# Recurrent attention and gated block on one core: four steps of 3072 TensorE instructions, one turn by DMA, extra rows in 8, 1 and 7

## Chip, core and metric

One core of a Trainium2 chip runs the kernel. The metric is the device time of one execution in microseconds. Execution times are given as the median of several runs with the lowest and the highest. A profile is one further execution, whose own time stands beside its span.

## What is computed

A sequence of 2048 rows of 640 values goes through a layer norm, a recurrent attention with a small memory, and a gated two-layer block. The attention works through 64 segments of 32 rows, and the first 8 output rows of a segment are the memory that the next one begins with:

```python
for s in range(n_seg):                       # 64 segments of 32 rows
    h = concat([mem, xs], axis=1)            # 8 memory rows + 32 rows
    q, k, v = (einsum('btd,dhe->bhte', h, W) for W in (Wq, Wk, Wv))   # 32 heads of 128
    p = softmax(where(mask, einsum('bhqe,bhke->bhqk', q, k) * scale, -1e9))
    o = einsum('bhte,hed->btd', einsum('bhqk,bhke->bhqe', p, v), Wo)
    mem = o[:, :M]; outs.append(o[:, M:])
...
h  = x + attention(layernorm(x))
h2 = h + ((relu_gate(xn @ W_gate) * (xn @ W_up)) @ W_down)            # xn = layernorm(h)
```

## The kernel before

The program is recorded as a list of operations with the tiles that they read and write (class `_Graph`), a pass works out the semaphore waits, and each engine then runs its own operations in the order in which they were recorded. So the order of the source is the order of each engine's queue. Bank conflicts in PSUM count as dependencies too.

The 64 segments are the steps `s` of one loop. The 8 memory rows and 24 of the 32 rows make one block of 32 rows (`act_r`); the last 8 rows of four segments are put together into another block of 32 rows (`act_e`), whose K, Q and V products are made once per four steps as filler ("extra units", three of the four steps), and whose output products (`woe_pass`, the extra rows' Wo passes) fill the step with s%4 = 1.

Weights are the moving operand. `project` (line 365) multiplies one block of 32 rows by half of a weight matrix, 2048 columns: five chunks of the 640 input values, and for each chunk four products of 512 columns, `g` = 0 to 3, one on each quarter (32 columns) of the TensorE array, one PSUM quarter each. `pe.matmul` issues a weight load (the block of 32 rows is the stationary operand) and a product; `again` (line 357) issues the product alone, with the weights that are still in the quarter. With `held` the first chunk of a pass uses `again`, because the pass before ended with the same chunk: the second half of K and of Q goes through the chunks backwards (`WAYS`, line 925), and V begins with the chunk that Q ended with.

One step records, on TensorE, in this order: K in two halves (P2, P3); `pv_x` (line 646) of the step before, the products of the 24 and extra rows with the values; Q in two halves (P0, P1); V's first half with the `scores` (line 456) of the first half of the heads between its chunks; V's second half with the other scores; `pv_mem` (line 511) for the memory rows of the first half; the filler's first part; `pv_mem` of the second half; the filler's second part; `wo_split` (line 570), the Wo pass over the first half of the heads, with 320 columns per product; `wo_pass` (line 557) over the second half, with 160 columns; the filler's last part. DVE and ACT then turn the result into the next step's memory rows (`fold_split`, `to_act_split`), and the next step's K reads them.

In the steps with s%4 = 1 the filler is `woe_pass`, 16 groups of four products of 320 columns, cut by `WPARTS` (line 778) into 7, 2 and 7 groups. In the same steps the next 128 layer-normed rows are turned: `flip_rows` (line 345) issues a DMA transpose on SyncE's queue into `at`, and GpSimd copies the pieces into `act_r` and `act_e` (`ln1_back`, line 415). In step 57 only 64 rows are left; there `ln1_trans` (line 412) turns them with five TensorE transposes into a PSUM bank, and ACT copies them to `at`.

Ahead of the loop the first step's Wo passes go group by group as the pieces of Wo arrive. `keep_busy` (line 873) records products whose result nobody reads (16 per call with argument 4, on the quarters in turn) between them.

Of the kernel before, what the change touches and what calls it, by code (L numbers as in the profile page):

```python
# [26 lines left out]
class _Graph:  # L27
# [10 lines left out]
    def add(self, eng, fn, r=(), w=(), dma=False):  # L38
        if eng == "pool" and not dma:
            r, w = tuple(r) + (("pool",),), tuple(w) + (("pool",),)  # L40
        op = _Op(eng, fn, tuple(r), tuple(w), dma)
        self.ops.append(op)
        return op
# [120 lines left out]
def build_kernel(nc, A_x, A_mem0, A_Wq, A_Wk, A_Wv, A_Wo, A_seg_len, B_W_gate, B_W_up, B_W_down, out):  # L164
    _, S, D = A_x.shape
# [6 lines left out]
    DC = D // 128  # L172
# [22 lines left out]
    W = ar.alloc("W", [128, 3, DC, HD], BF16)  # L195
# [52 lines left out]
    xl = ar.alloc("xl", [128, D], BF16)  # L248
    at = ar.alloc("at", [128, D], BF16)
# [6 lines left out]
    def bank(b):  # L256
        return ps[:, b * 512:(b + 1) * 512]

    def bank_bf(b):
        return ps[:, b * 512:(b + 1) * 512].bitcast(BF16)  # L260

    BQ = (0, 1)
    T0, T1 = 2, 3
    P0, P1, P2, P3 = 4, 5, 6, 7
# [10 lines left out]
    def B(n):  # L275
        return ("B", n)
# [7 lines left out]
    for i in range(2):  # L284
        add("dve", lambda v, i=i: v.memset(oT[i][:], 0.0), w=[("oT", i, n, kh) for n in "mx" for kh in range(2)])
        add("pool", lambda p, i=i: p.memset(act_r[i][:], 0.0),
            w=[("act", i, j, "m") for j in range(4)] + [("act", i, "x")] + [("act", i, "x", j) for j in range(4)])
# [6 lines left out]
    for g in range(4):  # L294
        for j in range(4):
            for r in range(2):
                sl, n = mca[32 * g:32 * g + 32, j, r, :], 0 if r == g % 2 else 1 + j
# [47 lines left out]
    def flip_rows(dst, src, skey, dkey):  # L345

        add("sp", lambda e: e.dma_start_transpose(dst, src[:, :]), r=[skey], w=[dkey], dma=True)

    def transpose_rows(src, skey, n, b):
        def f(pe):  # L350
            for c in range(DC):
                i = pe.matmul(bank_bf(b)[:, c * 128:c * 128 + n], src[0:n, c * 128:(c + 1) * 128], ident[0:n, 0:n],
                              is_transpose=True)
            return i
        add("pe", f, r=[skey, ("ident",)], w=[B(b)])

    def again(pe, dst, lhsT, rhs, start, stop, g):

        return pe.add_instruction(mybir.InstMatmult(  # L359
            name=nc.get_next_instruction_name(), engine=mybir.EngineType.PE,  # L360
            ins=[pe.lower_ap(rhs), pe.lower_ap(lhsT)], outs=[pe.lower_ap(dst)], start_tensor_calc=start,
            stop_tensor_calc=stop, tile_size=(128, 32 if g is not None else 128), tile_position=(0, 32 * (g or 0)),
            bass_skip_group_check=True, ldweights=False))

    def project(act, akeys, j, halves, banks, chunks=range(5), ends=(0, DC - 1), held=False):
        swap = 1 if j == 2 and akeys[0][0] == "acte" else 0

        def f(pe):
            for c in chunks:
                for n, i in enumerate(halves):  # L370
                    for g in range(4):
                        o = 2048 * i
                        w = (W[:, j, c, o + 512 * (g ^ swap):o + 512 * (g ^ swap) + 512] if j == 2 else
                             W[:, j, c, o:o + 2048].rearrange("p (h e) -> p h e", e=128)[:, :, 32 * g:32 * g + 32])
                        a = (bank(banks[n])[32 * g:32 * g + 32, :], act[:, c, :], w)
                        if n == 0 and not (held and c == chunks[0]):
                            ins = pe.matmul(*a, start=(c == ends[0]), stop=(c == ends[1]), skip_group_check=True)  # L377
                        else:
                            ins = again(pe, *a, c == ends[0], c == ends[1], g)
            return ins  # L380
        add("pe", f, r=list(akeys) + [("W", j, c) for c in chunks], w=[B(b) for b in banks] + [("Wdone", j)])
# [17 lines left out]
    def copy_op(eng, dst, src, r, w):  # L399
        if eng == "act":  # L400
            add("act", lambda a: a.activation(dst, src, ACTF.Copy), r=r, w=w)  # L401
        else:
            add("dve", lambda v: v.tensor_copy(dst, src), r=r, w=w)

    def n_rows(b):
        return 64 if b < 0 else min(128, S - 64 - 128 * b)
# [5 lines left out]
    def ln1_trans(b, buf, key, bk):  # L412
        transpose_rows(buf, key, 64 if b < 0 else min(128, S - 64 - 128 * b), bk)
# [20 lines left out]
    def chunks_of(flat):  # L434
        return flat.rearrange("p (c t) -> p c t", t=128)
# [4 lines left out]
    def pass_act(s):  # L440
        p, j = place(s)
        return act_r[p][:, j], [("act", p, j, "m"), ("act", p, "x", j), ("act", p, "x")]
# [297 lines left out]
    xe, xke = act_e[0], [("acte", 0)]  # L740
# [34 lines left out]
            w=[(("Wg", "Wu")[n], g, lo)], eng=eng)  # L775

    PARTS = (((0, (0, 1)), (1, (0, 1)), (2, (0,))), ((2, (1,)),), ((3, (0, 1)), (4, (0, 1))))
    WPARTS = (range(0, 7), range(7, 9), range(9, 16))

    def extra_units(s):  # L780
        p, r = 1 - place(s)[0], place(s)[1]
# [88 lines left out]
        add("dve", lambda v: v.tensor_tensor(hT[par][:, j, :], g1[gi][:, :], bank(bu), ALU.mult),  # L870
            r=[B(bu), ("g1", gi)], w=[("hT", par, j)])

    def keep_busy(n):

        def f(pe):
            for g in range(4 * n):
                o = 32 * (g % 4)
                i = pe.matmul(bank(T1)[o:o + 32, :], xe[:, 0, :], W[:, 2, 0, 0:512], start=True, stop=True,
                              skip_group_check=True)
            return i  # L880
        add("pe", f, r=xke + [("W", 2, 0)], w=[B(T1)])

# [25 lines left out]
    for g in range(4):  # L908
        wo_pairs(0, T0, g)
        if g:  # L910
            keep_busy(4)
    fold_split(T0, "pool")
    for g in range(3):
        wo_pass(0, P3, (1,), (g,))
# [7 lines left out]
    row_stats(xl, ("xl",), n_rows(1))  # L922
    row_scale(xl, ("xl",), n_rows(1), xl, ("xl",))

    WAYS = ((range(DC),), (range(DC - 1, -1, -1), (DC - 1, 0), True))

    for s in range(1, NSEG):
        last = s == NSEG - 1
        par = s % 2
        nb = s // 4 + 1  # L930
# [8 lines left out]
        def filler(n):  # L939
            if units:  # L940
                units(n)
            if woe:
                woe_pass(BQ[0], WPARTS[n])
        if s > 0:
            a, ks = pass_act(s)
            for i in range(2):
                project(a, ks, 1, (i,), ((P2, P3)[i],), *WAYS[i])
                to_tok((P2, P3)[i], i, "act")
                if last and i == 1:
                    load_piece(("Ko", 0), "act")  # L950
                flip(i, Ko, i, [("Ko", i)])
            if s % 4 == 2 and more:
                row_std(n_rows(nb + 1))
                row_scale(xl, ("xl",), n_rows(nb + 1), xl, ("xl",), "pool")
            if s % 4 == 1 and e2 is not None:
                row_std(128)
                row_scale(xt, ("xt",), 128, xt, ("xt",), "pool")
            pv_x(s - 1, 0)
            norm_x(0)
            if s % 4 == 0 and e2 is not None:  # L960
                add_attn(xt[:, :], xt, at, [("xt",), ("at",), ("rx",)], [("xt",)], "pool")
                dma(h_d[128 * e2:128 * e2 + 128, :], xt[:, :], r=[("xt",)], w=[("h_d", e2)])
            if s % 4 == 2:
                merge_v(s, 1)
            if not last:
                for i in range(2):
                    project(a, ks, 0, (i,), ((P0, P1)[i],), *WAYS[i])
                    to_tok((P0, P1)[i], 2 + i, "act")
                    flip(2 + i, Qo, i, [("Qo", i)])
                    if i == 0:  # L970
                        norm_x_late(0)
                        flip_ox(s - 1, (0,))
            else:
                norm_x_late(0)
                flip_ox(s - 1, (0,))
            if s == NSEG - 2:
                dma(xn2T[0][:, :, :], xn2_d[:, :, :], r=[("xn2_d", u) for u in range(4)] + [("Wdone", 0)],
                    w=[("xn2", 0, u) for u in range(4)])
            project(a, ks, 2, (0,), (P2,), range(4), held=not last)
            scores(s, 0, (0, 1))  # L980
            project(a, ks, 2, (0,), (P2,), (4,))
            scores(s, 0, (2, 3))
            if not last:
                exp_mem(s, 0)
                mask_mem(s, 0)
            to_v(P2, Vp, 0, ("Vp",), "act")
            if last:
                load_piece(("Vp", 0), "act")
            if s % 4 == 1 and ln:
                if n_rows(nb) == 128:  # L990
                    flip_rows(chunks_of(at[:, :]), xl, ("xl",), ("at",))
                else:
                    ln1_trans(nb, xl, ("xl",), BQ[1])
                if more:
                    ln1_load(nb + 1, xl, ("xl",))
        if last:
# [38 lines left out]
        if s == NSEG - 2:  # L1035
            p = 1 - place(s + 1)[0]
            add("pool", lambda o, p=p: o.tensor_copy(Qo[:, :, M:32], Qe[p][:, :, M:32]), r=[("Qe", p, i) for i in range(2)],
                w=[("Qo", i) for i in range(2)])
        if s > 0 and not woe and s != NSEG - 3:
            late_o(s - 1)  # L1040
        if s % 4 == 1 and ln:
            n = n_rows(nb)
            if n < 128:
                copy_op("act", chunks_of(at[:, :])[:, :, 0:n], chunks_of(bank_bf(BQ[1])[:, 0:D])[:, :, 0:n], [B(BQ[1])],
                        [("at",)])
            ln1_back(nb, chunks_of(at[:, :]), [("at",)], "pool")
        mask_x(s)
        if e2c is not None:
# [24 lines left out]
        if s == NSEG - 4:  # L1073
            p, j = place(NSEG - 1)
# [76 lines left out]
    s = NSEG - 1  # L1151
# [131 lines left out]
```

## Time and profile before

| what | value |
|---|---|
| median of 3 runs | 1007.59 us |
| lowest, highest | 1006.82, 1009.36 us |
| profiled execution, its own time | 1006.39 us |
| its span | 1004.7 us |
| TensorE clock granted | full in all slices |
| L377, products of 512 columns with `act_r` | 6832, 447.4 us busy |
| L565, Wo pass, 160 columns | 4032, 82.3 us busy |
| L582, Wo pass by pairs, 320 columns | 2016, 79.8 us busy |
| L625, extra rows' Wo passes | 1024, 44.0 us busy |
| L654, `pv_x` | 2048, 26.9 us busy |
| L878, `keep_busy` | 72, 5.1 us busy |

Times of the profile count from the start of the span. Busy time counts overlapping products once. PE stands for the products and PEld for the weight loads of TensorE. A row of the timeline is a run of equal instructions: start, duration from the first start to the last end, engine, line, operation, tiles, count, and in brackets the idle time of the engine ahead of it with what ended it. "issue" there means that the engine waited for nothing that the profile shows.

### The profile page before, as it was taken

Reading aid. Unit: us, or ns where it says so; the run is one execution under the profiler, and the core shown is the slowest. Engines: PE = TensorE matmul, PEld = TensorE weight load, DVE = VectorE, ACT = ScalarE, POOL = GpSimd, SP = SyncE. Lnnn points to the kernel's source line nnn. Section 1 sums busy time; section 2 is a strip of 40 time slices with the busy share of each in tenths; the row PEclk is TensorE's granted clock in tenths of the full one; section 3 lists DMA queues with packets and bytes.
Section 4 is the critical chain, followed back from the end, with each engine's and each line's share of the span. In section 5 each row is a group of like instructions: output and inputs, shape, how many; then the busy total and the mean of one; then the engine's idle time right before and its main releaser. Section 6 shows DMA issues by size and latency. Waiting matters only on the chain.

```text
span 1004.7 us, 53813 instructions
## 1 busy us (share of the span) xinstructions
PE 971.1 (97%) x25153; PEld 495.7 (49%) x23308; DVE 712.9 (71%) x1863; ACT 524.7 (52%) x1331; POOL 167.4 (17%) x416
## 2 busy tenths in 40 slices
PE   3789999999999999999999999999999999999998
PEld 0245555555555554555555555555555555344443
DVE  2568787878878887888788878787878765445332
ACT  0456566556666666666666666665656643122121
POOL 7020202121302130222022212111110010000000
PEclk9999999999999999999999999999999999999999
DMA  9931212121212111121212131211111158413100
GB/s 373 418 102 28 53 28 55 33 55 50 53 41 54 49 53 47 47 54 47 53 41 63 47 55 40 41 41 38 40 29 40 38 165 251 108 20 92 27 14 26
DMA packets 72421, 73.01 MB, mean 73 GB/s; under 512 B 41632, under 2 KB 59008, under 8 KB 70272
## 3 DMA queue, kind: packets, MB, share of 16 engines
q1 hardware_dynamic: 70064, 68.27, 23.6%
q8 instruction: 190, 3.11, 1.3%
q10 hardware_dynamic: 2128, 1.31, 0.5%
q14 instruction: 39, 0.32, 0.1%
HBM read 37.04 MB, written 6.55 MB: 43 GB/s over the span
## 4 chain that ended last, share of the span: by engine, by line
PE 93%; SPq 3%; DMA 2%; issue 1%; DVE 1%; ACT 0%; POOL 0%; DVEq 0%; ACTq 0%
PE ps L377 43%; PE ps L841 11%; PE ps L359 10%; PE ps L565 7%; PE ps L582 6%; PE ps L625 4%; SPq L324 3%; PE ps L1088 3%; PE ps L466 2%; PE ps L654 2%; DMA Wo<-in_A_Wo_dram 2%; PE ps L519 2%; PE ps L854 0%; PE ps L1100 0%; DVE TBf L605 0%
## 5 line engine op out<-in xcount | busy, mean ns | idle before, releaser
L377 PE MATMUL ps<-W,act_r 128*32 128x512 bf16 x6832 | 447.4, 380 | 3.1 <-DVE act_r L606 1.8
L377 PEld LDWEIGHTS ps<-W,act_r 128*32 128x32 bf16 x6832 | 169.7, 96 | 212.0 <-issue 63.1
L401 ACT ACTIVATE tok<-ps 128x512 bf16<-128x512 f32 x190 | 109.3, 594 | 57.3 <-PE ps L377 48.8
L377 PE MATMUL ps<-W,act_e 128*32 128x512 bf16 x1224 | 120.0, 383 | 8.0 <-DMA W<-in_A_Wv_dram 3.7
L396 DVE STREAM_TRANSPOSE Ko<-tox 128x512 bf16<-128x512 bf16 x128 | 89.8, 703 | 42.7 <-ACT tox L401 41.5
L474 POOL COPY Qo<-Qe 128x256 bf16<-128x256 bf16 x64 | 28.0, 437 | 528.9 <-DVE oT L539 521.0
L401 ACT ACTIVATE tox<-ps 128x512 bf16<-128x512 f32 x134 | 79.6, 598 | 56.5 <-PE ps L377 35.5
L545 DVE STREAM_TRANSPOSE oT<-tox 128x512 bf16<-128x512 bf16 x128 | 89.8, 702 | 0.0
L396 DVE STREAM_TRANSPOSE Qo<-tok 128x512 bf16<-128x512 bf16 x124 | 85.6, 690 | 0.9
L565 PE MATMUL ps<-Wo,oT 128*32 128x160 bf16 x4032 | 82.3, 233 | 2.8 <-DMA Wo<-in_A_Wo_dram 1.7
L359 PE MATMUL ps<-W,act_e 128*32 128x512 bf16 x856 | 84.6, 385 | 0.0
L582 PE MATMUL ps<-Wo,oT 128*32 128x320 bf16 x2016 | 79.8, 299 | 0.5 <-DVE rm L529 0.5
L359 PE MATMUL ps<-W,act_r 128*32 128x512 bf16 x808 | 79.9, 382 | 0.0
L565 PEld LDWEIGHTS ps<-Wo,oT 128*32 128x32 bf16 x4032 | 71.8, 97 | 12.0 <-DMA Wo<-in_A_Wo_dram 2.8
L401 ACT ACTIVATE Vp<-ps 128x512 bf16<-128x512 f32 x127 | 75.2, 592 | 0.5 <-ACT Vp L401 0.5
L869 ACT ACTIVATE g<-ps 128x512 bf16<-128x512 f32 x52 | 30.1, 593 | 79.5 <-PE ps L841 79.5
L595 ACT ACTIVATE SA<-TA 64x40 f32<-64x40 f32 x126 | 29.5, 234 | 77.0 <-DVE TA L593 76.2
L841 PE MATMUL ps<-xn2T,Wu 128*128 128x512 bf16 x259 | 64.5, 379 | 0.1
L870 DVE TENSOR_TENSOR hT<-g,ps 128x512 bf16<-128x512 bf16 x52 | 35.7, 687 | 40.6 <-PE ps L841 38.6
L482 ACT ACTIVATE Pm<-ps 128x64 bf16<-128x64 f32 x126 | 28.1, 223 | 69.2 <-PE ps L466 69.2
L841 PE MATMUL ps<-xn2T,Wg 128*128 128x512 bf16 x247 | 61.8, 379 | 1.3 <-issue 1.0
L582 PEld LDWEIGHTS ps<-Wo,oT 128*32 128x32 bf16 x2016 | 53.9, 97 | 16.0 <-DVE rm L529 1.2
(116 smaller groups left out, 1463.1 us busy)
## 6 DMA issues: line engine op xcount, KB each, us to landing
VM<-Vp SPq DMA_DIRECT2D x126, 65.0 KB
VM<-Vp SPq DMA_DIRECT2D x63, 130.0 KB
W<-in_A_Wk_dram SPq DMA_DIRECT2D x5, 1024.0 KB
W<-in_A_Wq_dram SPq DMA_DIRECT2D x5, 1024.0 KB
W<-in_A_Wv_dram SPq DMA_DIRECT2D x5, 1024.0 KB
Wo<-in_A_Wo_dram SPq DMA_DIRECT2D x8, 640.0 KB
attn_d<-wtok SPq DMA_DIRECT2D x248, 7.5 KB
xt<-in_A_x_dram SPq DMA_DIRECT2D x16, 160.0 KB
```

The source lines that it names most:

```text
L324: add(eng, lambda e: e.dma_start(dst, src), r=r, w=w, dma=True)
L359: return pe.add_instruction(mybir.InstMatmult(name=nc.get_next_instruction_name(), engine=mybir.EngineType.PE, ins=[pe.lower_ap(rhs), pe.l ...
L377: ins = pe.matmul(*a, start=(c == ends[0]), stop=(c == ends[1]), skip_group_check=True)
L396: add("dve", lambda v: v.transpose(dst[:, 16 * i:16 * i + 16, 0:32], tok[t][:, :].rearrange("p (h f) -> p h f", f=32)), r=tok_keys(t), w=keys)
L401: add("act", lambda a: a.activation(dst, src, ACTF.Copy), r=r, w=w)
L545: add("dve", lambda v, kh=kh: v.transpose(ap(oT[p], 160 * kh + M, [[320, 4], [40, 4], [1, 32]]), ap(tox, 128 * kh, [[256, 4], [1, 4], [4, ...
L565: i = pe.matmul(bank(bk)[32 * gg:32 * gg + 32, 0:160], src[:, hb, 0:32], w[:, gg], start=(hb == CH[16 * halves[0]]), stop=(hb == CH[-1]), ...
L582: i = pe.matmul(bank(bk)[32 * q:32 * q + 32, 0:320], src[:, hb, 0:32], w, start=(n == 0), stop=(n == 7), skip_group_check=True)
L625: ins = pe.matmul(bank(bk)[32 * q:32 * q + 32, 0:320], src[:, hb, 0:32], w[:, 2 * (q % 2):2 * (q % 2) + 2], start=(i == 0), stop=(i == 15) ...
L841: ins = pe.matmul(bank(bk), w[:, c, lo:lo + 128], xn2T[par][:, c, :], start=(c == 0), stop=(c == DC - 1))
L870: add("dve", lambda v: v.tensor_tensor(hT[par][:, j, :], g1[gi][:, :], bank(bu), ALU.mult), r=[B(bu), ("g1", gi)], w=[("hT", par, j)])
L1088: i = pe.matmul(*a, start=(j == 0), stop=(j == FC - 1), skip_group_check=True)
```

## The change

`project` gets an argument `parts`: so many instructions are added to the pass by dividing products of 512 columns into two of 256 columns, one right after the other on the same quarter. Where two or more are left to add, the second half has its own weight load (two instructions more); where one is left, it uses `again`. The pass's first chunk is not divided. `fill_of(s)` gives the number of instructions that are added in a step, 56, 39, 8 and 52 for s%4 = 0, 1, 2, 3, with other numbers for steps 1, 57, 61, 62 and 63: four at a time are added by leaving out `held` (weights are loaded again for the first chunk of a pass), up to three passes; the rest are divided products, spread over the two halves of K and the two of Q. V's passes and the units of the extra rows have no divided products. Four steps then have 3072 TensorE instructions, where they had 2917.

Three of the calls of `keep_busy` ahead of the loop issue their 16 products in 2, 2 and 4 narrower pieces each, so that the loop begins at another place of the instruction stream. `WPARTS` becomes 8, 1 and 7 groups. Step 57 turns its rows with `flip_rows` as the other steps do, and its ACT copy goes.

```diff
-    def project(act, akeys, j, halves, banks, chunks=range(5), ends=(0, DC - 1), held=False):
+    def project(act, akeys, j, halves, banks, chunks=range(5), ends=(0, DC - 1), held=False, parts=0):
         swap = 1 if j == 2 and akeys[0][0] == "acte" else 0

         def f(pe):
+            left = parts
             for c in chunks:
                 for n, i in enumerate(halves):
                     for g in range(4):
...
                         if n == 0 and not (held and c == chunks[0]):
-                            ins = pe.matmul(*a, start=(c == ends[0]), stop=(c == ends[1]), skip_group_check=True)
+                            k = min(left, 2) if c != ends[0] else 0
+                            left -= k
+                            for q in range(2 if k else 1):
+                                b = a if not k else (a[0][:, 256 * q:256 * q + 256], a[1],
+                                                     w[:, 256 * q:256 * q + 256] if j == 2 else w[:, 8 * q:8 * q + 8])
+                                if q and k == 1:
+                                    ins = again(pe, *b, c == ends[0], c == ends[1], g)
+                                else:
+                                    ins = pe.matmul(*b, start=(c == ends[0]), stop=(c == ends[1]), skip_group_check=True)
                         else:
                             ins = again(pe, *a, c == ends[0], c == ends[1], g)
...
-    WPARTS = (range(0, 7), range(7, 9), range(9, 16))
+    WPARTS = (range(0, 8), range(8, 9), range(9, 16))
...
-    def keep_busy(n):
+    def keep_busy(n, cut=1):
+        wide = 512 // cut
...
-                i = pe.matmul(bank(T1)[o:o + 32, :], xe[:, 0, :], W[:, 2, 0, 0:512], start=True, stop=True,
-                              skip_group_check=True)
+                for q in range(cut):
+                    i = pe.matmul(bank(T1)[o:o + 32, 0:wide], xe[:, 0, :], W[:, 2, 0, 0:wide], start=True, stop=True,
+                                  skip_group_check=True)
...
         if g:
-            keep_busy(4)
+            keep_busy(4, (1, 2, 2, 4)[g])
...
-    WAYS = ((range(DC),), (range(DC - 1, -1, -1), (DC - 1, 0), True))
+    WAYS = ((range(DC), (0, DC - 1)), (range(DC - 1, -1, -1), (DC - 1, 0)))
+    FILL = (56, 39, 8, 52)
+
+    def fill_of(s):
+        n = {1: 31, 57: 39, 61: 39, 62: 50, 63: 0}.get(s, FILL[s % 4])
+        alone = min(n // 4, 3)
+        rest = n - 4 * alone
+        return [k < 3 - alone for k in range(3)], [2 * ((rest // 2 + k) // 4) + (k == 0 and rest % 2) for k in range(4)]
...
+            held, parts = fill_of(s)
             for i in range(2):
-                project(a, ks, 1, (i,), ((P2, P3)[i],), *WAYS[i])
+                project(a, ks, 1, (i,), ((P2, P3)[i],), *WAYS[i], held=i == 1 and held[0], parts=parts[i])
...
-                    project(a, ks, 0, (i,), ((P0, P1)[i],), *WAYS[i])
+                    project(a, ks, 0, (i,), ((P0, P1)[i],), *WAYS[i], held=i == 1 and held[1], parts=parts[2 + i])
...
-            project(a, ks, 2, (0,), (P2,), range(4), held=not last)
+            project(a, ks, 2, (0,), (P2,), range(4), held=not last and held[2])
...
-                if n_rows(nb) == 128:
-                    flip_rows(chunks_of(at[:, :]), xl, ("xl",), ("at",))
-                else:
-                    ln1_trans(nb, xl, ("xl",), BQ[1])
+                flip_rows(chunks_of(at[:, :]), xl, ("xl",), ("at",))
...
-            n = n_rows(nb)
-            if n < 128:
-                copy_op("act", chunks_of(at[:, :])[:, :, 0:n], chunks_of(bank_bf(BQ[1])[:, 0:D])[:, :, 0:n], [B(BQ[1])],
-                        [("at",)])
             ln1_back(nb, chunks_of(at[:, :]), [("at",)], "pool")
```

## The prediction

> **What bounds the kernel now.** I read the page first: engines, queues, the chain of waits.
>
> ```profile
> PE 971.1 (97%) x25153; PEld 495.7 (49%) x23308; DVE 712.9 (71%) x1863; ACT 524.7 (52%) x1331; POOL 167.4 (17%) x416
> q8 instruction: 190, 3.11, 1.3%
> PE 93%; SPq 3%; DMA 2%; issue 1%; DVE 1%; ACT 0%; POOL 0%; DVEq 0%; ACTq 0%
> ```
>
> TensorE is the bound: 97% busy, 93% of the chain. Its 25153 recorded products and 23308 weight loads over the 190 packets of q8 are 255 instructions a packet, 16 KB each: TensorE's program comes in pieces of 256 instructions.
>
> Then the timeline: L654 runs once a step, so its starts mark the recurrence.
>
> ```profile
> 59.30 0.31 PE L654 MATMUL ps<-VM,Px 64*32 64x129 bf16 x16
> 302.06 0.36 PE L654 MATMUL ps<-VM,Px 64*32 64x129 bf16 x23
> 350.31 0.35 PE L654 MATMUL ps<-VM,Px 64*32 64x129 bf16 x21
> 653.56 0.35 PE L654 MATMUL ps<-VM,Px 64*32 64x129 bf16 x21
> 703.25 0.36 PE L654 MATMUL ps<-VM,Px 64*32 64x129 bf16 x24
> 788.03 0.36 PE L654 MATMUL ps<-VM,Px 64*32 64x129 bf16 x24
> ```
>
> From 302.06 to 350.31 four steps take 48.25 us; from 653.56 to 703.25 the same work takes 49.69. From 59.30 to 788.03 are 15 such stretches: 728.73 us, against 15 x 48.26 = 723.9. So 4.8 us are lost unevenly. The timeline shows where:
>
> ```profile
> 445.01 0.40 PE L377 MATMUL ps<-W,act_e 128*32 128x512 bf16 x4 [0.41 <-issue]
> ...
> 700.71 0.45 PE L625 MATMUL ps<-Wo,oTe 128*32 128x320 bf16 x7 [0.65 <-issue]
> ```
>
> TensorE waits for nothing that another engine does ("issue"). In the list of its instructions 15360 = 60 x 256 lie between these two places: both are the first of a piece. The other such gaps sit on the same grid, where the piece before was run through in about 3.5 us or less. A stretch has 2917 instructions, 101 over 11 x 256, so the grid wanders and only some stretches are hit.
>
> **The change, part by part.**
>
> *Fixed pieces.* Stretches become 3072 = 12 x 256 instructions, three pieces a step. On the built list a piece begins about 2.3 us (L654), 6.3 to 6.7 us (late V products) and 10.2 us (second Wo pass) into each step. That takes away the wandering waits, at most -4.8 us. The shortest piece, V to Wo pass in steps s%4 = 1, lasts 3.4 us. Where a piece lay like that before (steps 5, 17, 25, 37, 45) the wait was 0.42, 0.31, 0.13, 0.11 and 0 us, mean 0.19; as the stage also gets shorter (below) I take 0.23, x 15 = +3.5 us, bounds 0 and 15 x 0.42 = 6.3.
>
> The Trainium skill ("Runtime: NRT & Kernel Launch", Instruction fetch mechanics) has the same 256-instruction blocks, and says that crossing one costs a queue bump that is mostly hidden. By that the two terms would be nothing and the sum 1.3 us higher; the gaps of 0.41 and 0.65 us disagree.
>
> *Weights loaded again.* 44 loads per stretch return where `held` had left them out. The four rows of 40 columns below issue 8 instructions in 25 ns, 3 ns each; four products of 512 columns take 216 ns, which hides four loads. I take 0; uncovered 44 x 3 ns x 15.5 = 2 us.
>
> *Divided products.* This term decides. 22, 14, 0 and 20 products per stretch (s%4 = 0, 1, 2, 3) become two halves of 256 columns, **the second right after the first, on the same quarter of the array**.
>
> ```profile
> 59.65 1.26 PE L377 MATMUL ps<-W,act_r 128*32 128x512 bf16 x20
> ...
> 305.44 0.19 PE L466 MATMUL ps<-Qo,Ko 128*32 128x40 bf16 x4
> 305.46 0.19 PE L466 MATMUL ps<-Qo,Ke 128*32 128x40 bf16 x4
> 305.49 0.19 PE L466 MATMUL ps<-Qo,Ko 128*32 128x40 bf16 x4
> 305.51 0.19 PE L466 MATMUL ps<-Qo,Ke 128*32 128x40 bf16 x4
> ...
> 850.77 1.24 PE L841 MATMUL ps<-xn2T,Wu 128*128 128x512 bf16 x5
> 851.85 1.26 PE L854 MATMUL ps<-xn2T,Wt 128*128 128x256 bf16 x10
> ```
>
> Twenty quarter products are 5 groups of four: (1.26 - 0.39) / 4 = 0.216 us a group, so four quarters run together when they follow each other in turn. On one place, 512 columns take (1.24 - 0.38) / 4 = 0.215 and 256 columns (1.26 - 0.272) / 9 = 0.110 us: h = 0.109 per half. No row has two quarter products in a row on one quarter. From below: if the other quarters pass by, a divided product costs 2 x 0.110 - 0.216, 4 ns, some 0.4 us in all. From above: products start in program order, so quarter 1 can start only once quarter 0's second half has, h later. A group with all four divided has its starts at 0, h, 2h, 3h, and the next group begins at 4h instead of 2h; the last quarter stays h behind, which is paid at the next change of layout or the next short products. With three divided: the next begins at 3h, 2h of lag. Divisions beyond the fourth cost only their lag. So (K pair + Q pair): s%4 = 3, 5h + 5h; s%4 = 0, 5h + 6h; s%4 = 1, 5h + 4h. 30h = 3.27 us a stretch; x 15, with 16h for steps 1 and 62, 466h = 50.8 us.
>
> Which end? The x4 rows speak for order: 40 columns need 17 ns at 216 per 512, but four products come every 25 ns, with the quarter order 0 1 2 3, 1 0 3 2; and loads keep that order: in step 9 quarter 0's product starts at 159.965, but its next load only at 159.970, 3 ns behind quarter 1's. Everything seen of TensorE is in turn, so I take the upper end, **+50.8**.
>
> The Trainium skill ("TensorE: Matmul & The Clock Gate", Part 3, row/col tiling) says it outright: "MATMULs are pc-monotone in start AND end — strict FIFO, no reordering"; only weight loads are pulled ahead. By it the term is 50.8, without it 0.4. No run here has shown it on one quarter yet.
>
> *Start.* Three fillers of 16 products are cut in 2, 2 and 4 on one quarter: 17h, 17h and about 2.7 us instead of 0.86 each, +3.7 us. Behind them come Wo passes that wait for their load, as here, four times, 1.7 us in all:
>
> ```profile
> 50.77 0.46 PE L565 MATMUL ps<-Wo,oT 128*32 128x160 bf16 x16 [0.37 <-DMA Wo<-in_A_Wo_dram]
> ```
>
> So +2.0; 0 if quarters pass each other, 3.7 without that cover.
>
> *Extra rows 8, 1, 7.* In steps s%4 = 1 one group of L625 (0.136 us) moves ahead of the second pv_mem, which waits:
>
> ```profile
> 162.52 0.10 PEld L519 LDWEIGHTS ps<-Ve,Pbd 128*32 128x32 bf16 x4 [0.33 <-DVE Pbd L488]
> ...
> 163.53 0.31 DVE L539 STREAM_TRANSPOSE oT<-om 128x128 bf16<-128x128 bf16 x1 [0.49 <-ACT om L531]
> 163.90 1.18 PEld L565 LDWEIGHTS ps<-Wo,oT 128*32 128x32 bf16 x64
> ```
>
> TensorE is idle there some 0.15 us, so the group is hidden. The split pass follows 0.136 earlier, but the Wo pass (L565) needs L539, done at 163.84: its loads at 163.90 already come right behind it, and its products start at 164.00. About 0.08 us is won: 14 x 0.08 = -1.1 us (0 to -1.9). Without the cover it would only be a swap, 0.
>
> *Step 57.* Five 64-row transposes and two changes of layout leave TensorE, a copy leaves ACT, one DMA transpose (14 like it, 1.25 us on SP's queue) goes ahead of three VM loads and the step's small stores, as in the other s%4 = 1 steps, which take 12.17 us against 12.53 here: -0.3 us. If it came late, the POOL copies for step 58 would wait up to the 1.25.
>
> *Sum* against the profiled execution, 1006.39 us (span 1004.7 and 1.7 around it): -4.8 + 3.5 + 0 + 50.8 + 2.0 - 1.1 - 0.3 = +50.1, 1056.5. The median of the runs is 1.2 above that execution: **1057 us** (rounded down for waits that a slower TensorE absorbs). Its own range, from the bounds: 1050 to 1062.
>
> **Rivals.**
> - *Only the loads keep order*; products of other quarters pass. Each divided product then holds the next quarter by one load and its start, 25 ns (x4 rows): 75 ns a pair, 0.15 a step, 46 steps: +6.9. 1006.4 + 6.9 - 4.8 + 3.5 - 1.1 - 0.3 + 1.2 = 1012. For: only loads are seen to be held. Against: nothing shows a product overtaking.
> - *Quarters are independent and no piece waits* (faster). +0.4 for divisions, waits -4.8 and none left: 1006.4 + 0.4 - 4.8 - 1.1 - 0.3 + 1.2 = 1002. It decides as soon as a half does not hold the other quarters. For: the 48.25 stretches show that no wait is needed. Against: the 25 ns rows.
> - *The pieces do not do what they should*: a fixed grid that meets a dense place meets it 15 times. At 0.65 us (700.71) that is +9.8 on the faster case, 1011. For: every stretch is alike now. Against: no piece is under 3.4 us.
>
> **How the numbers follow.** Forecast 0.58, faster case 0.18, loads alone 0.17, bad grid 0.07. The likeliest gives 1057. Leaving out the ends of the forecast and half of the faster case, 8 in 10 need 1002 to 1062; the middle is nearly empty. A measurement of this kernel tells 0.3% (3 us) from no change. Faster: most of the faster case and a tail of the loads case, 0.18; same: 0.09; slower: 0.73.
>
> **What would show it.** Right: the L377 rows split into 512 and 256 columns, and K and Q passes of a step grow by about half a microsecond a pair; steps s%4 = 2 stay at 12.03 us while s%4 = 0 and 3 take about 13.2. Fixed grid: "issue" gaps vanish or sit at one place of every s%4 = 1 step. Extra rows: the wait before L519 shrinks there. Wrong: the steps with divisions stay near 12.1 us, or a step s%4 = 2 becomes longer too.

## The result, and the profile after

The changed kernel takes 1004.69 us at the median (1003.56 to 1006.76, 8 runs), the kernel before on the same chip 1007.39 us: ratio 0.9974, 95% interval 0.9965 to 0.9984. Beside the kernel before on another chip (experiment e5_after) it was 1005.30 against 1005.94 us, 0.9991 (0.9980 to 1.0001). So it is 2.7 us faster in the first measurement; the 0.6 us of the second are within its noise, as the interval reaches past 1. Forecast were 1057 us.

The profiled execution took 1004.47 us, with a span of 1002.7. Its page has the engines, the queue of instruction pieces and the chain:

```profile
PE 970.9 (97%) x26097; PEld 537.8 (54%) x24920; DVE 715.6 (71%) x1863; ACT 524.9 (52%) x1330; POOL 167.8 (17%) x416
q8 instruction: 200, 3.28, 1.4%
PE 93%; DMA 3%; SPq 2%; DVE 1%; issue 1%; ACT 0%; POOL 0%; DVEq 0%; ACTq 0%
```

The changed kernel has 944 products and 1612 weight loads more and fetches ten pieces more (q8 carries them), and TensorE is as busy as it was. In the timeline, L663 is what L654 was, `pv_x`, once a step:

```profile
60.60 0.42 PE L663 MATMUL ps<-VM,Px 64*32 64x129 bf16 x32
302.24 0.42 PE L663 MATMUL ps<-VM,Px 64*32 64x129 bf16 x32
350.47 0.42 PE L663 MATMUL ps<-VM,Px 64*32 64x129 bf16 x32
652.44 0.42 PE L663 MATMUL ps<-VM,Px 64*32 64x129 bf16 x32
700.67 0.42 PE L663 MATMUL ps<-VM,Px 64*32 64x129 bf16 x32
785.06 0.42 PE L663 MATMUL ps<-VM,Px 64*32 64x129 bf16 x32
```

From 302.24 to 350.47 and from 652.44 to 700.67 four steps take 48.23 us both times (before: 48.25 and 49.69). The 15 stretches take 724.46 us against 728.73. What TensorE waited for between 75 and 790 us, first the kernel before (what is waited for; us in total, times, longest):

```profile
PE ps L625 <- issue: 1.0, 2, 0.7
PE ps L377 <- issue: 0.6, 2, 0.4
PE ps L377 <- DVE act_r L606: 0.5, 3, 0.2
PE ps L565 <- issue: 0.2, 1, 0.2
```

and the changed kernel, which has one row left:

```profile
PE ps L386 <- DVE act_r L615: 0.5, 3, 0.2
```

The waits for a piece ("issue") are gone. The view leaves out the shorter gaps; the whole is seen in the length of the steps, from the first K load of one to that of the next:

| step | before, no wait in it | after |
|---|---|---|
| s%4 = 0 | 12.027 us | 12.067 us |
| s%4 = 1 | 12.180 us | 12.092 us |
| s%4 = 2 | 12.030 us | 12.029 us |
| s%4 = 3 | 12.023 us | 12.042 us |
| step 53, with a wait | 13.25 us | 12.10 us |
| step 57 | 12.53 us | 12.04 us |

Over the whole span, from the same loads:

| part of the span | before | after | difference |
|---|---|---|---|
| start, to the first K load of step 1 | 57.03 us | 58.33 us | +1.30 |
| steps 1 to 61 | 740.84 us | 736.58 us | -4.26 |
| step 62 to the end | 206.80 us | 207.84 us | +1.04 |

So 2.3 of the 4.3 us won in the loop are given back at its two ends. At the start the timeline of the changed kernel shows what took the place of four waits for Wo (1.7 us in all), a wait of 1.50 us for a piece. It also shows that TensorE doesn't follow the forecast's rule:

```profile
51.14 0.83 PE L889 MATMUL ps<-W,act_e 128*32 128x128 bf16 x39
53.47 0.47 PE L889 MATMUL ps<-W,act_e 128*32 128x128 bf16 x19 [1.50 <-issue]
53.74 0.25 PE L574 MATMUL ps<-Wo,oT 128*32 128x160 bf16 x2
53.77 0.23 PE L889 MATMUL ps<-W,act_e 128*32 128x128 bf16 x2
53.81 0.23 PE L574 MATMUL ps<-Wo,oT 128*32 128x160 bf16 x1
53.82 0.22 PE L889 MATMUL ps<-W,act_e 128*32 128x128 bf16 x1
```

L889 is `keep_busy`, L574 the Wo pass behind it. In the program all 64 L889 products of this call come first, sixteen times four pieces on one quarter. Here L574 starts at 53.74 and 53.81 and L889 again at 53.77 and 53.82: a product of one quarter starts ahead of older products of another.

### The profile page after: what moved, and what is told of

Read it like the earlier page. It is cut to its first block, busy times and chain, and to the rows that moved or that the text cites. A ratio compares the mean times of both kernels' runs of the same rounds, so it can differ in the third digit from the quotient of the medians.

```text
span 1002.7 us, 56369 instructions
## 1 busy us (share of the span) xinstructions
PE 970.9 (97%) x26097; PEld 537.8 (54%) x24920; DVE 715.6 (71%) x1863; ACT 524.9 (52%) x1330; POOL 167.8 (17%) x416
## 4 chain that ended last, share of the span: by engine, by line
PE 93%; DMA 3%; SPq 2%; DVE 1%; issue 1%; ACT 0%; POOL 0%; DVEq 0%; ACTq 0%
PE ps L386 47%; PE ps L850 10%; PE ps L359 7%; PE ps L574 7%; PE ps L591 7%; PE ps L634 4%; PE ps L1100 3%; DMA W<-in_A_Wv_dram 3%; PE ps L475 2%; PE ps L663 2%; PE ps L528 2%; SPq L324 1%; DMA Wd<-in_B_W_down_dram 0%; PE ps L889 0%; PE ps L863 0%
## 5 line engine op out<-in xcount | busy, mean ns | idle before, releaser
L386 PE MATMUL ps<-W,act_r 128*32 128x512 bf16 (+1 forms) x8369 | 454.4, 358 | 2.9 <-DVE act_r L615 1.8
L386 PEld LDWEIGHTS ps<-W,act_r 128*32 128x32 bf16 x8369 | 212.9, 96 | 168.3 <-DVE act_r L615 33.1
L554 DVE STREAM_TRANSPOSE oT<-tox 128x512 bf16<-128x512 bf16 x128 | 94.2, 736 | 0.0
L359 PE MATMUL ps<-W,act_e 128*32 128x512 bf16 x856 | 85.5, 387 | 0.0
L574 PE MATMUL ps<-Wo,oT 128*32 128x160 bf16 x4032 | 82.4, 233 | 0.9 <-issue 0.9
L574 PEld LDWEIGHTS ps<-Wo,oT 128*32 128x32 bf16 x4032 | 71.4, 97 | 9.7 <-DVE oT L548 3.1
L548 DVE STREAM_TRANSPOSE oT<-om 128x128 bf16<-128x128 bf16 x126 | 39.1, 310 | 31.1 <-ACT om L540 31.1
```

The lines of the kernel that those rows point to most:

```text
L359: return pe.add_instruction(mybir.InstMatmult(name=nc.get_next_instruction_name(), engine=mybir.EngineType.PE, ins=[pe.lower_ap(rhs), pe.l ...
L386: ins = pe.matmul(*b, start=(c == ends[0]), stop=(c == ends[1]), skip_group_check=True)
L548: add("dve", lambda v: v.transpose(ap(oT[par], 160 * hf, [[40, 4], [320, 4], [1, 8]]), ap(om, 128 * hf, [[1, 4], [4, 32]])), r=[("om", hf) ...
L554: add("dve", lambda v, kh=kh: v.transpose(ap(oT[p], 160 * kh + M, [[320, 4], [40, 4], [1, 32]]), ap(tox, 128 * kh, [[256, 4], [1, 4], [4, ...
L574: i = pe.matmul(bank(bk)[32 * gg:32 * gg + 32, 0:160], src[:, hb, 0:32], w[:, gg], start=(hb == CH[16 * halves[0]]), stop=(hb == CH[-1]), ...
```

## The experiments

**One part alone.** e1_grid has only the pieces:

```diff
-    WPARTS = (range(0, 8), range(8, 9), range(9, 16))
+    WPARTS = (range(0, 7), range(7, 9), range(9, 16))
-        n = {1: 31, 57: 39, 61: 39, 62: 50, 63: 0}.get(s, FILL[s % 4])
+        n = {1: 31, 57: 29, 61: 39, 62: 50, 63: 0}.get(s, FILL[s % 4])
...
+                if n_rows(nb) == 128:
+                    flip_rows(chunks_of(at[:, :]), xl, ("xl",), ("at",))
+                else:
+                    ln1_trans(nb, xl, ("xl",), BQ[1])
```

> Left as in the kernel before: the extra rows' passes in 7, 2 and 7 groups, and step 57's rows turned by TensorE (their instructions taken off that step's filling, so that a piece still begins where it does in the changed kernel). So only the fixed pieces remain: divided products, weights loaded again, cut fillers at the start. Theory A (quarters pass each other; the whole gain is the wandering waits, and the divisions cost about 1 us): steps s%4 = 0 and 3 stay at 12.04 to 12.07 us, no wait by 'issue' after step 1, and the time is about 1.8 us under the kernel before and 1.2 to 1.6 us over the changed one: 1006. Rival B (the divisions do cost, and 8/1/7 with step 57 paid for them): 1008 or more, over the kernel before.

e2_others is the kernel before with only these two edits the other way, `WPARTS` in 8, 1 and 7 and `flip_rows` in step 57:

> The kernel before with only the extra rows' passes in 8, 1 and 7 groups and step 57's rows turned by DMA; no product divided, no weights loaded again, no filler cut. Theory A: 0.08 to 0.09 us in each of 14 steps and 0.35 to 0.5 us in step 57, 1.5 to 1.7 us under the kernel before; the wandering waits stay (gaps by 'issue' of 0.3 to 1.05 us at places that change from stretch to stretch). Rival B: 3 us under it, as much as the whole change brings.

Measured: e1_grid 1006.58 us, ratio 1.0007 (0.9998 to 1.0016); e2_others 1004.45 us, 0.9993 (0.9984 to 1.0002), the kernel before 1005.81 us. The totals separate neither theory: e1_grid is no faster than the kernel before, as rival B said, and theory A's 1.8 us under it did not come. The traces do. In e1_grid steps s%4 = 1 take 12.188 us where the whole change has 12.092, and step 57 takes 12.53 against 12.04: extra rows 0.096 x 14 = 1.3 us, step 57 0.49 us. Steps s%4 = 0, 2 and 3 are those of the changed kernel (12.063, 12.029, 12.041), and from step 2 to 61 it takes 726.04 us against 728.76 before: 2.7 us won there by the pieces alone, with the divisions paid. It loses them outside: its start takes 59.13 us instead of 57.03, with this row among its waits at the start:

```profile
PE ps L889 <- issue: 2.4, 1, 2.4
```

In e2_others s%4 = 1 steps without a wait take 12.083 us, 0.097 less than before, step 57 12.03, and the wandering waits are there (12.76 us in step 13, 12.65 in step 33).

**The places of the pieces.** e3_shift moves every piece by 88 instructions:

```diff
-        n = {1: 31, 57: 39, 61: 39, 62: 50, 63: 0}.get(s, FILL[s % 4])
+        n = {1: 119, 57: 39, 61: 39, 62: 50, 63: 0}.get(s, FILL[s % 4])
```

> The changed kernel with 88 more instructions in step 1 (119 instead of 31 filled in), so that every later piece begins 88 instructions earlier in its step. By the trace of the changed kernel its shortest pieces would then be run through in 2.93 and 3.16 us instead of 3.27. Theory A (a piece is late when the one before is run through faster than its successor is fetched, and the fetch starts 0 to 1.2 us after a piece begins, takes 1 us and needs 1.3 us more): a wait by 'issue' returns at one or two places of the s%4 = 1 steps, in most stretches, 0.1 to 0.6 us: +1.5 to +5 us over the changed kernel. Rival C (where pieces begin doesn't matter; the waits went for another reason): no change, within 0.5 us.

Measured: 1018.18 us, ratio 1.0115 (1.0099 to 1.0131). Its waits between 75 and 790 us, and one place of its timeline:

```profile
PE ps L634 <- issue: 5.5, 10, 0.9
PE ps L386 <- DVE act_r L615: 0.5, 3, 0.2
```

```profile
316.74 0.31 PE L634 MATMUL ps<-Wo,oTe 128*32 128x320 bf16 x2 [0.86 <-issue]
```

The wait sits where theory A had it: s%4 = 1 steps take 12.24 to 13.11 us, at the median 12.78 instead of 12.09, s%4 = 2 steps 12.15 instead of 12.03, the other two kinds are unchanged at the median (three steps s%4 = 3 take 0.15 us more). Rival C falls. But steps 2 to 61 grow by 10.1 us, twice theory A's upper end. The size was wrong, as I read it, because I looked at one piece at a time. Here two short pieces follow each other (2.97 and 3.16 us by the changed kernel's speed; about 6.1 together). In none of the six traces of e1 to e4, before and after do two fetches in the loop start less than 3.23 us apart, and only one in twenty less than about 3.4 to 3.5. A single short piece between long ones is covered by the lead that its fetch has; the second in a row has none left. By that it waits 2 x 3.4 - 6.1 = 0.7 us, and these steps grew by 0.69 us at the median. This account was made after the run, and no later run tests it. The rest of the difference lies behind step 62, 3.5 us, 2.5 of it in a wait for Wd; why that load was late there stays open.

**The start.** e4_spread has the same pieces from step 2 on and no dense filler:

```diff
-            keep_busy(4, (1, 2, 2, 4)[g])
+            keep_busy(4)
...
-        keep_busy(1)
+        keep_busy(1, (2, 2, 4)[g])
...
-    keep_busy(3)
+    keep_busy(3, 2)
...
-        n = {1: 31, 57: 39, 61: 39, 62: 50, 63: 0}.get(s, FILL[s % 4])
+        n = {1: 127, 57: 39, 61: 39, 62: 50, 63: 0}.get(s, FILL[s % 4])
```

> The changed kernel with the same pieces from step 2 on, but the instructions that move them are not put into the three dense runs of fillers at the start: those are whole again, and 64 cuts go into the later, smaller fillers and 96 instructions into step 1. Theory A: the wait by 'issue' of 1.5 us in the fillers goes; the four Wo passes there wait for their load again, up to 1.7 us in all as in the kernel before. So 0 to 1.3 us faster than the changed kernel: 1003.5 to 1004.7. Rival D (the clock at half speed for 6 us at the start is caused by the dense fillers too): another 1 us less, 1003.

It was run again beside the changed kernel itself (e6_spread, e5_after):

> The changed kernel once more, unaltered, beside the next two on one chip: about 0.9974 of the kernel before.

> The kernel of e4_spread again, beside the changed kernel: theory A 0 to 1.3 us faster than it; rival (the dense fillers' wait is paid anyway by the waits for Wo) no difference.

Measured: e4_spread 1003.06 us, 0.9976 (0.9965 to 0.9986); then e5_after 1005.30 us, 0.9991 (0.9980 to 1.0001) where 0.9974 was expected, and e6_spread 1002.97 us, 0.9964 (0.9952 to 0.9976): 2.3 us faster than the changed kernel at the median. Among e4_spread's waits at the start stands what stood there before (in e6_spread, the same kernel, it is one wait of 0.3 us):

```profile
PE ps L574 <- DMA Wo<-in_A_Wo_dram: 1.6, 4, 0.5
```

The five profiles with dense fillers (after, e1, e3, e5, e9) reach step 1 at 57.64 to 59.13 us, mean 58.2, with one wait for a piece of 1.4 to 2.45 us; the two of e4 and e6 at 57.62 and 57.22 (e7, e10 and e11 at 57.08 to 57.63), before at 57.03. So about 0.8 us are explained, and theory A's 1.3 at most. The fillers alone don't make that wait: in the changed kernel's profile the piece ahead of it began at 47.75 us and ran 4.2 us, longer than many in the loop, but the fetch that was due then started only at 51.02, with the DMA engines fully busy (share 1.02 from 46 to 53 us), and landed at 52.12. The other part of the 2.3 us, and why the changed kernel's runs spread from 1003.19 to 1007.11 and these only from 1002.01 to 1003.62, is not. Rival D falls: a stretch at half clock (four products of 512 columns in 0.62 instead of 0.40 us; granted clock 0.55 to 0.60 from 42 to 50 us in the changed kernel) is in the profiles of e6_spread at the same place and of e10_far from 37.6 us too, which have no dense filler. In e1_grid, which has them, it comes at 52.5 us. The kernel before has none in its profile, so a part of the changed kernel's 1.3 us at the start may be the clock; e6_spread, with as long a stretch, is at step 1 after 57.22 us.

**Order of the quarters.** e8_order puts blocks of products that do nothing else ahead of step 1, each behind a read of the bank by VectorE:

```diff
+    def turns(n, total=64):
+        return [q for _ in range(total // (4 * n)) for q in range(4) for _ in range(n)]
+    def quarter(q, n):
+        return bank(T1)[32 * q:32 * q + 32, 0:n], xe[:, 0, :], W[:, 2, 0, 0:n]
...
+    for f in (lambda pe: [pe.matmul(*quarter(q, 512), **KW) for q in turns(1)][-1],
+              lambda pe: [pe.matmul(*quarter(q, 256), **KW) for q in turns(2)][-1],
+              lambda pe: [pe.matmul(*quarter(q, 512), **KW) for q in turns(2)][-1],
+              lambda pe: [pe.matmul(*quarter(q, 512), **KW) for q in turns(4)][-1],
+              lambda pe: [pe.matmul(*quarter(q, 512), **KW) for q in turns(16)][-1],
+              lambda pe: held_turns(pe, 1),
+              lambda pe: held_turns(pe, 4),
+              lambda pe: held_turns(pe, 16)):
+        add("pe", f, r=xke + [("W", 2, 0)], w=[B(T1)])
+        add("dve", lambda v: v.tensor_copy(st[:, 0, :], bank(T1)[:, 0:6]), r=[B(T1)], w=[("st", 0)])
```

> The changed kernel with eight blocks of products put in before step 1, each block alone on TensorE (it waits until VectorE has read the bank). All but the second have 64 products of 512 columns, 16 for each quarter of the array. In turn 0 1 2 3 they take 16 x 0.216 = 3.46 us. Order of the quarters, each product with its load: runs of 1; runs of 2 halves of 256 columns (64 halves, 1.75 us if free); runs of 2; runs of 4; runs of 16. Then with the load left out after a quarter's first product: runs of 1, 4 and 16. Theory A (each quarter takes its products in its own order, none waits for another quarter): 3.5, 1.8, 3.5, and about 3.5 to 5 for runs of 4 and 16, as far as TensorE looks ahead; without loads at least as fast. Rival (my forecast's step: every product starts after the one before it in the program, so a run of n lets the next quarter start n - 1 products later): 3.5, 3.5, 6.9, 10.4, 13.0 us, and the same without loads: 3.5, 10.4, 13.0.

The five blocks with a load for each product, in its timeline (start, duration):

```profile
59.64 3.82 PE L949 MATMUL ps<-W,act_e 128*32 128x512 bf16 x64
63.72 1.94 PE L950 MATMUL ps<-W,act_e 128*32 128x256 bf16 x64 [0.26 <-DVE st L958]
65.94 3.65 PE L951 MATMUL ps<-W,act_e 128*32 128x512 bf16 x64 [0.29 <-DVE st L958]
69.88 3.68 PE L952 MATMUL ps<-W,act_e 128*32 128x512 bf16 x64 [0.29 <-DVE st L958]
73.86 11.45 PE L953 MATMUL ps<-W,act_e 128*32 128x512 bf16 x64 [0.31 <-DVE st L958]
```

and the last block, runs of 16 without loads; L945 is the first product of each quarter, L359 the others:

```profile
93.39 0.39 PE L945 MATMUL ps<-W,act_e 128*32 128x512 bf16 x1 [0.28 <-DVE st L958]
95.35 0.39 PE L945 MATMUL ps<-W,act_e 128*32 128x512 bf16 x1
97.31 0.39 PE L945 MATMUL ps<-W,act_e 128*32 128x512 bf16 x1
99.27 0.39 PE L945 MATMUL ps<-W,act_e 128*32 128x512 bf16 x1
```

Two halves in a row on one quarter take 1.94 us for 64 where order would take 3.5; two or four whole products in a row take 3.65 and 3.68 us, as little as products in turn (3.82, and 3.64 without loads), where order would take 6.9 and 10.4. Without loads runs of four take 3.65 us and runs of 16 take 9.50, where order would take 10.4 and 13.0. The rival, my forecast's step, is refuted directly. Theory A was too bold at the other end: runs of 16 take 11.45 us, not 3.5 to 5. The last fence shows how far TensorE looks ahead: quarter 1 starts 1.96 us after quarter 0, when quarter 0's tenth product has begun (9 x 0.216 = 1.94) and six of the sixteen still wait. With loads the next quarter's first load comes at 2.605 us, right behind quarter 0's thirteenth product, with three products and two loads waiting. So in these two blocks five or six waiting instructions are passed, and no more.

**More divisions at the same count.** e9_alldiv:

```diff
-        alone = min(n // 4, 3)
+        alone = 0
```

> The changed kernel with no weights loaded again: the 44 loads of a stretch are replaced by 22 more divided products (28, 20, 4 and 26 in the steps s%4 = 0, 1, 2 and 3 instead of 22, 14, 0 and 20), so that every piece begins at the same count as before. Theory A (quarters pass each other; 8 halves begin in 218 ns where 4 products begin in 216): steps of 12.03 to 12.11 us as now, each within 0.02 us, s%4 = 2 too. Rival (my forecast's step, a half holds up the other quarters, 0.109 us each time): four divided products cost 2 x 0.109 more, 22 of them 1.2 us a stretch on top of what the first 56 cost, and steps s%4 = 2 grow by 0.2 to 0.5 us.

Measured: one run of 1003.95 us. The steps take 12.041, 12.122, 12.034 and 12.070 us (s%4 = 0 to 3; the changed kernel 12.067, 12.092, 12.029 and 12.042), together 0.04 us a stretch more for 22 more divisions, against the rival's 1.2. Each kind stays within 0.03 us, a little more than the 0.02 expected. The changes have both signs, so the few hundredths that s%4 = 0 and 3 took on are no price for one division or one load; what sets them stays open.

**Step 62.** Behind the loop's regular part one wait for a piece stood in most profiles. e7_far was to take it away by moving all pieces 12 instructions:

```diff
-        n = {1: 127, 57: 39, 61: 39, 62: 50, 63: 0}.get(s, FILL[s % 4])
+        n = {1: 139, 57: 39, 61: 39, 62: 50, 63: 0}.get(s, FILL[s % 4])
```

> As e4_spread, and 12 more instructions in step 1 (139), so that every later piece begins 12 instructions earlier in its step. By the trace of e4_spread no piece from step 2 to the last step but one is then run through in less than 3.5 us, where the shortest are now 3.27 us in the s%4 = 1 steps and 3.11 us in step 62. Theory A (what counts is how fast pieces follow each other; no two fetches have begun less than 3.23 us apart in any run): nothing changes in steps 2 to 61, which wait for nothing already (two waits of 0.02 us); the wait before the Wo pass of step 62, 0.92 us in the changed kernel's profile, goes in every run: 0.3 to 1 us faster than e4_spread at the median, and the runs lie closer together. Rival C (the places don't matter): no difference to e4_spread.

Measured: 1003.07 us, 0.9966 (0.9954 to 0.9978), the same as e6_spread, as rival C said. Steps 2 to 61 didn't change, as both expected, but the wait that theory A took away stayed, 0.87 us, though the piece ahead of it lasts 3.6 us without it. The next kernel was made from e7_far's trace, where the engines' busy times and the share of the DMA engines' time (last but one) around it are:

```profile
800.00:804.00 4.00, 4.00 (x168) 2.71 (x164) 3.29 (x12) 2.57 (x8) 0.00 (x0) 1.00 0.81 242
```

```profile
804.34 0.25 PE L574 MATMUL ps<-Wo,oT 128*32 128x160 bf16 x2
805.45 1.22 PE L574 MATMUL ps<-Wo,oT 128*32 128x160 bf16 x60 [0.87 <-issue]
```

e11_tail moves one load:

```diff
-            if s == NSEG - 2:
-                dma(xn2T[0][:, :, :], xn2_d[:, :, :], r=[("xn2_d", u) for u in range(4)] + [("Wdone", 0)],
-                    w=[("xn2", 0, u) for u in range(4)])
...
         if s == NSEG - 2:
             load_piece(("om", 0))
+            dma(xn2T[0][:, :, :], xn2_d[:, :, :], r=[("xn2_d", u) for u in range(4)] + [("Wdone", 0)],
+                w=[("xn2", 0, u) for u in range(4)])
```

> The kernel of e7_far again, beside the next: 0.9966 of the kernel before.

> As e7_far, but in step 62 the load of xn2T (640 KB) is issued after the first Wg piece and the first Wu piece instead of ahead of them. In e7_far's trace the fetch for the piece that begins before the Wo pass is due when a piece begins at 800.78 and starts only at 803.06, while that load and the next fill the DMA engines (busy share 0.75 to 0.87 from 800 to 804 us); the Wo pass then waits 0.9 us. Theory E (a fetch stands behind the program's large loads): the fetch starts within 1.2 us of the piece's beginning, and step 62 takes 12.1 to 12.3 us instead of 13.05: 0.5 to 0.9 us faster than e10_far. Rival F (the fetch is late for another reason, or the load of xn2T then arrives late for the first gate product): no gain, or a wait for xn2T before that product.

Measured: e10_far 1002.84 us, 0.9961 (0.9947 to 0.9975); e11_tail 1002.23 us (1001.90 to 1003.52), 0.9956 (0.9943 to 0.9968). The same stretch and the Wo pass in e11_tail:

```profile
800.00:804.00 4.00, 4.00 (x162) 2.61 (x148) 3.29 (x13) 2.35 (x7) 0.00 (x0) 1.00 0.41 103
```

```profile
804.07 1.29 PE L574 MATMUL ps<-Wo,oT 128*32 128x160 bf16 x64
```

The DMA engines are half as busy there, the fetch starts 0.56 us after the piece began (801.07 against 800.51) instead of 2.28, and all 64 products run without a gap. Step 62 takes 12.19 us, against 12.66 in e10_far and 13.05 in e7_far. So this profile agrees with theory E; xn2T came in time. The 0.6 us between the medians is about what the traces say, though the two intervals overlap. One profile shows the same without the edit: in e4_spread the piece began 6.97 us into step 62, the fetch started at 7.13 and the step took 12.20 us, though the DMA engines were 0.83 busy from 800.41 to 804.41 us. There the load of xn2T was issued 5.79 us into the step; in the five other profiles with the pieces at the same places (after, e1, e5, e6, e9) it was issued at 5.03 to 5.56, and the fetch started at 8.6 to 9.3. That fits a fetch that got ahead of the load, and says that the busy share alone doesn't decide. e11_tail is the fastest of all these kernels: 4.3 us under the kernel before beside it (1006.48 us), where the changed kernel was 2.7 and 0.6 us under it.

## Why the prediction failed, step by step

- *Divided products, +50.8 us: the step that failed.* "A half holds up the other quarters" is not what TensorE does. e8_order shows each quarter running on in its own order, as long as no more than five or six instructions wait ahead of it; a divided product is four instructions. e9_alldiv shows the price in the kernel itself: 22 more divisions cost 0.04 us a stretch, where the forecast's rule gives 1.2. What the divisions and the loads added in the loop is the growth of the steps s%4 = 0 and 3, (0.040 + 0.019) x 15 = 0.9 us. The 25 ns rows of 40 columns, from which I argued order, show only how fast products of all four quarters can be started; no row had tested two in a row on one place. I named that gap, had a bound of 0.4 us below, and took the far end. The rival "quarters are independent and no piece waits", 1002 us, is what happened, 2.7 us too low.
- *Fixed pieces, -4.8 us: right in kind, measured about -3.5.* The 4.8 had counted two things that are no waits for pieces: 0.3 us at the end of each of three steps s%4 = 3, which wait for the next block of rows and still do (the one row of the waits above), and 0.35 us of step 57: 4.8 - 0.9 - 0.35.
- *A recurring wait in s%4 = 1, +3.5 us: nothing.* The piece lasts 3.27 us there, shorter than I had, and waits in two of 15 steps, 0.02 us each, because its neighbour lasts 4.4 us. e3_shift shows what a second short piece beside it costs: 10.1 us.
- *Weights loaded again, 0: right.* Steps s%4 = 2, which have only that, take 12.029 us as before.
- *Start, +2.0 us: measured +1.3, for another reason.* I had it from order on one quarter. What came is one wait for a piece, 1.5 us, because the fillers ran through 256 instructions in 4.2 us while the fetch started 3.3 us after they began; it stands in place of the waits for Wo.
- *Extra rows, -1.1 us: -1.3* (0.096 in each of 14 steps, between the whole change and e1_grid). *Step 57, -0.3 us: -0.49.*
- *Not foreseen:* +1.0 us behind step 62, from a wait for Wd of 0.54 and one for a piece of 0.42 us. e5_after, the same kernel, has neither of them and 1.06 us less from step 63 on, so this varies from run to run.

With the failed step at 0.9 and the recurring wait at 0, the forecast's own other terms give 1006.4 - 4.8 + 0.9 + 2.0 - 1.1 - 0.3 + 1.2 = 1004.3 us. That this comes so near is partly luck, because errors cancel: the gain from fixed pieces was 1.3 us too large, but the start cost 0.7 us less than forecast, the median lay 0.2 us above the profiled execution instead of 1.2, and 1.0 us at the end was not foreseen. The measured time lies at the lower end of the range, 1002 to 1062, in the part that it held for the rivals.

## What to carry to other kernels

Before a row is read as order, ask whether anything in it could have gone out of order: products in turn over the quarters look the same either way, and a block of 64 products, put alone on the engine, settles it. Fixing where instruction pieces begin is worth what the waits in the loop are worth (2.7 us here, of which e1_grid's total kept nothing), and only at places where, as here, no two pieces in a row are run through in less than about 3.4 us. Filling in should go where TensorE is slow or waits anyway, not into the densest products. A fetch can come late while the program's own large loads fill the DMA engines, so a load of 640 KB that isn't needed yet is worth trying later.

## What the runs showed of the hardware

- Products of different quarters pass each other: runs of four on one quarter cost nothing (3.68 against 3.82 us in turn), runs of 16 cost three times as much (11.45 us), and five or six waiting instructions are passed. The Trainium skill ("TensorE: Matmul & The Clock Gate", Part 3, row/col tiling) has products start and end strictly in program order; by that the runs of four would take 10.4 us (an estimate from 0.216 us for 512 columns). The trace disagrees.
- Fetches of 256 instructions started at least 3.23 us apart in the loop of six traces and took 0.9 to 1.8 us to land. By the Trainium skill ("Runtime: NRT & Kernel Launch", Instruction fetch mechanics) the cost of crossing a block is mostly hidden; the trace agrees for the changed kernel, whose pieces wait twice for 0.02 us in steps 2 to 61, and disagrees where two short pieces follow each other: the same program with its pieces 88 instructions earlier lost 10.1 us there.
- A fetch started 3.3 us after its piece began with the DMA engines at a busy share of 1.02 (the changed kernel at 51.02 us), 2.28 us after with 0.81 (e7_far) and 0.56 us after with 0.41 (e11_tail). In e4_spread it was 0.16 us with 0.83, so the share alone doesn't decide.
